# A spectral filter gated by an FFN on one Trainium2 core: slab 0 of x on the SP queue, its transposes and copies in two parts, and the statistics rows leaving from a corner of RB

## The chip, the core and the metric

The kernel runs on one core of a Trainium2 chip. A core has TensorE (PE, matmuls into PSUM; its weight loads are listed as PEld), VectorE (DVE), ScalarE (ACT), GpSimd (POOL) and SyncE (SP, which issues transfers). Each engine works through its own instructions in order, and engines wait for each other through semaphores. [...] The metric is the time on the device in microseconds (us), the median of several executions; one execution was also recorded by the profiler, and all durations come from that record.

## The reference

```python
x  = A_x                                   # 1 x 2048 x 640, bf16
xn = (x - mean(x)) / sqrt(var(x) + 1e-5)   # over the 640 columns
X  = rfft2(xn, axes=(-2, -1)) * (A_w_r + 1j * A_w_i)
s  = irfft2(X, s=(2048, 640)).astype(bf16)
f  = (gelu(xn @ w_gate) * (xn @ w_up)) @ w_down     # 640 -> 1536 -> 640, tanh form of gelu
return x + s * silu(f)
```

The branch s is a two-dimensional Fourier transform, a product with a complex weight and the way back. The branch f is a feed-forward network on the same normalised rows.

## The kernel before

x is cut into 16 slabs of 128 rows (row index n2*16 + n1: slab n1 holds every 16th row). The columns are transformed by products with cosine and sine tables, the 2048 rows as 128 x 16: a product with F1T per slab (L528), a round trip through DRAM (D2 to BU), a product with T2 (L649, L666), the row tables FM and FT (L686, L693), the weight product on VectorE (L725 to L736), and the same steps back (TI at L768, D3 to BU, I1T at L802, IT and IM at L820 and L826). The network works on four groups of 512 rows: for each of 12 column blocks a gate product into PSUM tile pg and an up product into pu (`gate_up`, L882), gelu on ACT (L899), the product of both on DVE into uT (L903), and then the down product (`down`, L966) with tanh, silu, the product with s and the sum with x.

**Who sets the order.** Nothing is scheduled by the hardware. Every step is a `Task` given to `Plan` (L115) with an engine or a choice of engines, a cost, a rank, the tasks that it comes after, and the rotating buffers (`Slot`) that it takes new or uses. `Plan.run` (L159) plays the tasks through in a simulated time, always taking the ready task of the lowest rank on a free engine, and the kernel then emits the instructions in that order. `BUFS` (L283) says how many buffers each kind has: `sp=2` PSUM tiles for transposes and transforms, `th=2`, and so on. `land` is the time at which the planner assumes that a transfer has landed. A change of costs or of `land` thus moves later instructions on all engines, though the code of those is the same.

**The start.** PE first multiplies ones by ones seven times (`keep_warm`, L362, L377) while the first loads run. Slab 0 of x is loaded from ACT's queue (L349); its task in the plan (L371) emits nothing and only carries its landing time. SP then issues slab 1, the first two column blocks of the gate weights Wg, slab 2, the first two blocks of the up weights Wu, slab 3, and the other weights, slabs and tables (L372 to L393, all by the helper at L303).

For the first group the rows are not waited for in normalised form. `turn_raw` (L452) transposes raw slabs 0 to 3 on PE, five 128 x 128 pieces each (L461), into one PSUM tile, and one copy (L463, recorded at L296, the line of `copy_on`) takes all five pieces to XR, which has a column of ones at place 128. The first two column blocks of the network (`early` in `gate_up`, L872) are computed from XR, first for slab 0 alone, with the ones column giving the column sums of the weights (WSUM); mean and 1/sigma are applied behind the product (L916, L918). Other blocks use the normalised rows xnT, transposed on PE for slabs 0 to 3 (`turn_pe`, L468) and by transfer from slab 4 on (`turn_dma`, L490).

**The statistics rows.** Mean and 1/sigma of slabs 0 to 3 stand as eight columns in RM. One transpose on PE (L560) makes eight rows of 128 of them in a PSUM tile; DVE copies these into a buffer `rt` of the kind `th` (L562); a transfer writes them to DRAM (D5, L563), and a second one reads D5 back to all 128 partitions of RB (L564). L916 and L918 read RB. Buffers of the kind `th` are also the place for the unused output of the statistics on ACT (`total` and `square`, L415 to L419) and for tanh at the end.

Of the kernel before, what the change touches and what calls it, by code (L numbers as in the profile page):

```python
# [11 lines left out]
FP32 = mybir.dt.float32  # L12
BF16 = mybir.dt.bfloat16
ACT = mybir.ActivationFunctionType
ALU = mybir.AluOpType
P = 128
S = 2048
D = 640
# [96 lines left out]
class Plan:  # L115
# [12 lines left out]
    def add(self, emit, eng, cost, rank, after=(), new=(), use=(), size=0, slow=1.0, hold=0, order=(), lag=0, land=0):  # L128
        engs = eng if isinstance(eng, dict) else {eng: cost}
        t = Task(emit=emit, engs=engs, rank=rank, after=list(after), new=list(new), size=size, slow=slow, hold=hold, order=list(order), lag=lag, land=land,  # L130
                 seq=len(self.tasks))
        for s in (*new, *use):
            s.users.append(t)
        self.tasks.append(t)
        return t
# [72 lines left out]
def c_pe(*ns):  # L208
    occ = sum(n / 2.4 + 2.5 for n in ns)
    return occ, occ + 240  # L210


def c_act(n, psum=True, extra=0):
    return 0.833 * n + 60 + extra, 0.833 * n + 200 + extra


def c_dve(n, rate=2, psum=False, extra=0):
    d = ((120 if psum else 58) + n / rate) / 0.96 + extra
    return d + 10, d + 130
# [3 lines left out]
def kernel(  # L223
# [11 lines left out]
    nc = tc.nc  # L235
    xv = A_x[0].rearrange("(n2 n1) d -> n2 n1 d", n1=NSLAB)
# [17 lines left out]
    ident = consts.tile([P, P], BF16)  # L254
# [7 lines left out]
    XR = persist.tile([P, 5, 513], BF16)  # L262
    RB = persist.tile([P, 2, 4, P], FP32)
    identF = consts.tile([P, P], FP32)
    RM = consts.tile([P, 2, 4], FP32)
    X = persist.tile([P, NSLAB, D], BF16, tag="xb", name="X")
    xnT = persist.tile([P, 5, S], BF16)
    Wg = persist.tile([P, 5, F], BF16)
    Wu = persist.tile([P, 5, F], BF16)
# [3 lines left out]
    D5 = dpool.tile([8, P], FP32)  # L273
# [12 lines left out]
    add = plan.add  # L286

    def place(slot, shape, dt=BF16):
        if slot.tag in ("sp", "pg", "pu"):
            slot.tile = psum.tile([P, *shape], dt, tag=slot.tag, name=slot.tag)  # L290
        else:
            slot.tile = work.tile([P, *shape], dt, tag=slot.tag, name=slot.tag, bufs=BUFS[slot.tag])
        return slot.tile

    def copy_on(e, out, in_):
        return nc.scalar.copy(out=out, in_=in_) if e == "ACT" else nc.vector.tensor_copy(out=out, in_=in_)  # L296
# [5 lines left out]
    def dma(out, in_, rank, size, after=(), new=(), use=(), slow=1.0, land=0):  # L302
        return add(lambda e: nc.sync.dma_start(out=out() if callable(out) else out, in_=in_() if callable(in_) else in_),  # L303
                   "SP", (430, 430), rank, after=after, new=new, use=use, size=size, slow=slow, land=land)

    gv = B_w_gate.rearrange("(c p) f -> p c f", p=P)
    uv = B_w_up.rearrange("(c p) f -> p c f", p=P)
    dv = B_w_down.rearrange("(t p) d -> p t d", p=P)
    sX = Slot("xb")
    sX.tile = X  # L310
    plan.slots["xb"].append(sX)
    x_in, g_in, u_in, tab_in, d_in = {}, {}, {}, {}, {}
# [3 lines left out]
    def load_x(a, b, land=0):  # L316
        seq[0] += 1
        t = dma(X[:, a:b, :], xv[:, a:b, :], (0, -4, seq[0]), (b - a) * 163840, use=[sX], land=land)
        for n in range(a, b):
            x_in[n] = t  # L320
# [9 lines left out]
    def load_w(sb, view, got, a, b, land=0):  # L330
        cs = slice(a * P, b * P)
        seq[0] += 1
        w = dma(sb[:, :, cs], view[:, :, cs], (0, -4, seq[0]), (b - a) * 163840, slow=1.1, land=land)
        for t in range(a, b):
            got[t] = w
# [10 lines left out]

    nc.gpsimd.memset(warm, 0.0)
    nc.vector.memset(mh, -0.5)
    nc.scalar.dma_start(out=X[:, 0, :], in_=xv[:, 0, :])  # L349
    nc.gpsimd.memset(ident, 0.0)  # L350
    nc.gpsimd.affine_select(out=ident, in_=ident, compare_op=ALU.not_equal, fill=1.0, base=0, pattern=[[-1, P]], channel_multiplier=1)
    nc.gpsimd.memset(XR[:, :, 128:129], 1.0)
# [9 lines left out]
    def keep_warm(n, after, rank=(0, -9), ns=425):  # L362
        def go(e):
            if heat.tile is None:
                place(heat, (2, 512))
            for k in range(n):
                nc.tensor.matmul(heat.tile[:, k % 2, :], lhsT=ones[:, 0:P], rhs=ones,  # L367
                                 start=True, stop=True, skip_group_check=True)
        return add(go, "PE", (n * ns, n * ns), rank, after=after, new=[] if heat.users else [heat], use=[heat] if heat.users else [])
    seq[0] += 1  # L370
    x_in[0] = add(lambda e: None, "SP", (1, 1), (0, -5), size=1, land=3620)  # L371
    load_x(1, 2, land=4150)  # L372
    load_w(Wg, gv, g_in, 0, 2, land=5210)
    load_x(2, 3, land=5700)
    load_w(Wu, uv, u_in, 0, 2, land=6760)
    load_x(3, 4, land=7250)
    t = warmed = keep_warm(7, [], ns=425)  # L377
    load_gu(2, 4)
    load_x(4, 6)
# [70 lines left out]
    raw, sums_out = {}, {}  # L450

    def turn_raw(n1):  # L452
        pt = Slot("sp")

        def half():
            return pt.tile[:, 0, :].bitcast(BF16)[:, 0:D]

        def mm(e):
            place(pt, (2, 512))
            for c in range(5):  # L460
                nc.tensor.transpose(out=half()[:, c * P:c * P + P], in_=X[:, n1, c * P:c * P + P], identity=ident)  # L461
        a = add(mm, "PE", c_pe(*[140] * 5), (0, n1), after=[x_in[n1], warmed], new=[pt], use=[sX])
        raw[n1] = add(lambda e: copy_on(e, XR[:, :, n1 * P + (n1 > 0):(n1 + 1) * P + (n1 > 0)], half().rearrange("p (c n) -> p c n", c=5)),  # L463
                      {"ACT": c_act(640)} if n1 < 1 else {"ACT": c_act(640), "DVE": (415, 560)}, None, (0, n1), after=[a], use=[pt], hold={0: 1000, 1: 1000}.get(n1, 200))
    for n1 in range(4):
        turn_raw(n1)

# [86 lines left out]
            fold(n1 // 2, [aps[n1 - 1], aps[n1]])  # L554


    sr, rt = Slot("sp"), Slot("th")

    def rows_pe(e):
        nc.tensor.transpose(out=place(sr, (2, 512))[0:8, 0, 0:P], in_=RM.rearrange("p k n -> p (k n)"), identity=identF)  # L560
    t = add(rows_pe, "PE", (215, 460), (0, 7), after=[*minused, turned[2]] + [roots[n1] for n1 in range(4)], new=[sr])
    t = add(lambda e: nc.vector.tensor_copy(out=place(rt, (P,), FP32)[0:8, :], in_=sr.tile[0:8, 0, 0:P]), "DVE", c_dve(128, 1, True), (0, 3.5), after=[t], new=[rt], use=[sr])  # L562
    rs = dma(D5, lambda: rt.tile[0:8, :], (0, -5, 0), 4096, after=[t], use=[rt])  # L563
    rb_in = dma(RB.rearrange("p k n t -> p (k n t)"), D5.rearrange("k t -> (k t)").partition_broadcast(P), (0, -5, 1), 524288, after=[rs])  # L564

    sB = Slot("xb")
# [23 lines left out]
    def rows(w, first, n, width):  # L590
        return bass.AP(tensor=w.tensor, offset=w.offset + first * L, ap=[[P * L, n], [1, width]])

    for ri, w in enumerate((A_w_r, A_w_i)):
        for G in range(8):
            b = 8 * G if G else 2
            turned_w[G].append(add(lambda e, ri=ri, w=w, G=G, b=b: nc.sync.dma_start(
                out=D4[:, b:8 * G + 8, ri, :], in_=bass.AP(tensor=w.tensor, offset=w.offset + (P - b) * L, ap=[[P * L, NSLAB], [-L, 8 * G + 8 - b], [1, LP]])),
                                   "SP", (650, 650), (2, G) if G < 2 else (3, G - 1.5), after=[turned[3]] if G < 2 else [B_in[3]], size=82432, slow=1.7))
        for a, n, b, first, width in ((0, 8, 0, 1088, LP), (8, 7, 0, 1152, LP), (15, 1, 0, 1024, LP), (0, 15, 1, P - 1, LP), (15, 1, 1, S - 1, L)):
            turned_w[0].append(add(lambda e, ri=ri, w=w, a=a, n=n, b=b, first=first, width=width: nc.gpsimd.dma_start(  # L600
                out=D4[a:a + n, b, ri, 0:width], in_=rows(w, first, n, width)), "POOL", (600, 600), (9, ri, b, a), after=[roots[15]], size=5152))
# [447 lines left out]
```

## Time and profile before

| what | value |
|---|---|
| median of 6 executions | 202.37 us (202.11 to 202.51) |
| the profiled execution | 202.31 us, of which 200.5 us are the span of its instructions |
| PE busy | 194.5 us (97%) |
| PEld, DVE, ACT, POOL busy | 118.0, 148.8, 127.1, 32.2 us |
| first and last matmul | 0.77 us; the last starts at 196.23 us |
| DMA | 32.62 MB, 163 GB/s on average over the span |

A row of the timeline or of a group reads: start, duration, engine, line, operation, output<-input, partitions x elements and type, number of instructions; in square brackets the idle time ahead of it and what ended that. A row of the waits reads: engine, what it was about to do, what it waited for, then the total in us, how often, and the longest. "PEq" is PE's own sequencer. The busy time of a matmul includes the end of its pipeline, so the time between two starts is the better measure of what one costs.

### The profile page before, as it was taken

How to read it: one execution, taken by the hardware profiler on the slowest of the kernel's cores; microseconds unless marked ns; L12 is line 12 of the kernel's file. 1: busy time of each engine (PE TensorE's matmuls, PEld its weight loads, DVE VectorE, ACT ScalarE, POOL GpSimd, SP SyncE). 2: the span in 40 equal slices, each digit the busy share in tenths (PEclk: the TensorE clock that was granted, in tenths of full speed). 3: DMA queues.
4: the chain of work that ended last, by engine and by line, in shares of the span. 5: the costliest groups of instructions: out<-in, count | busy, mean ns of one | idle time of the engine just before them, and what ended most of it. 6: DMA issues, size and time to landing. Idle time of an engine off the chain costs nothing.

```text
span 200.5 us, 4104 instructions
## 1 busy us (share of the span) xinstructions
PE 194.5 (97%) x1508; PEld 118.0 (59%) x1526; DVE 148.8 (74%) x321; ACT 127.1 (63%) x224; POOL 32.2 (16%) x71
## 2 busy tenths in 40 slices
PE   8999999999999999999999999999999999999991
PEld 3994444676444655777755455467755555457781
DVE  2898989997233159999998999933257789787774
ACT  3999879966432767777775667243466665675421
POOL 2605250697000000000000000000004022211210
PEclk9999999999999999999999999999999999999999
DMA  6999999899639767533234110117605243332432
GB/s 182 327 316 324 339 394 211 218 235 172 193 92 375 233 162 212 135 105 114 68 111 136 65 65 0 69 65 236 287 3 147 85 134 109 99 103 85 131 103 65
DMA packets 35894, 32.62 MB, mean 163 GB/s; under 512 B 10910, under 2 KB 32930, under 8 KB 35874
## 3 DMA queue, kind: packets, MB, share of 16 engines
q1 hardware_dynamic: 34434, 29.49, 50.1%
q0 software_dynamic: 1152, 2.66, 4.9%
q8 instruction: 12, 0.20, 0.4%
q10 hardware_dynamic: 288, 0.20, 0.3%
q14 instruction: 8, 0.07, 0.1%
HBM read 22.51 MB, written 9.19 MB: 158 GB/s over the span
## 4 chain that ended last, share of the span: by engine, by line
PE 96%; issue 1%; DVE 1%; ACT 0%; DVEq 0%
PE pu L882 26%; PE pg L882 25%; PE pg L966 13%; PE pu L966 13%; PE sp L693 3%; PE sp L826 3%; PE sp L768 2%; PE sp L802 2%; PE sp L666 2%; PE sp L528 2%; PE sp L367 2%; PE sp L686 1%; PE sp L820 1%; PE sp L461 1%; PE sp L474 1%
## 5 line engine op out<-in xcount | busy, mean ns | idle before, releaser
L882 PE MATMUL pu<-xnT,Wu 128*128 128x512 bf16 (+1 forms) x238 | 57.0, 365 | 0.4
L882 PE MATMUL pg<-xnT,Wg 128*128 128x512 bf16 (+1 forms) x234 | 56.5, 365 | 0.5
L903 DVE TENSOR_TENSOR uT<-pu,ge 128x512 bf16<-128x512 f32 x46 | 31.7, 690 | 20.0 <-PE pu L882 14.4
L966 PEld LDWEIGHTS <-uT 128*128 128x128 bf16 x396 | 37.8, 98 | 13.5
L899 ACT ACTIVATE ge<-pg 128x512 bf16<-128x512 f32 x46 | 27.5, 598 | 23.0 <-PE pg L882 22.2
L882 PEld LDWEIGHTS <-Wg 128*128 128x128 bf16 x285 | 25.4, 98 | 22.5 <-issue 0.3
L882 PEld LDWEIGHTS <-Wu 128*128 128x128 bf16 x285 | 24.9, 98 | 21.8
L966 PE MATMUL pg<-Wd,uT 128*128 128x320 bf16 (+2 forms) x204 | 30.7, 293 | 0.0
L966 PE MATMUL pu<-Wd,uT 128*128 128x320 bf16 (+1 forms) x192 | 29.7, 297 | 0.0
L296 ACT CAST ma<-sp 128x644 bf16<-128x644 f32 (+1 forms) x32 | 23.4, 794 | 9.7 <-PE sp L826 7.9
L928 POOL COPY xr<-s 1x1 bf16<-1x1 bf16 x1 | 0.2, 179 | 100.6 <-DVE s L852 100.6
L296 ACT CAST mc<-sp 128x640 bf16<-128x640 f32 x16 | 10.8, 696 | 5.0 <-DMA D<-mc 4.3
L929 POOL DMA_DIRECT2D xr<-in_A_x_dram x16 | 8.8, 550 | 32.3 <-DVE res L953 32.0
L975 ACT ACTIVATE th<-pu 128x320 f32<-128x320 f32 (+1 forms) x16 | 7.0, 437 | 10.9 <-PE pu L966 9.6
L980 DVE SCALAR_TENSOR_TENSOR G<-th,pg 128x320 bf16<-128x320 f32 (+1 forms) x16 | 7.7, 480 | 8.3 <-ACT th L975 8.2
L296 ACT CAST IU<-sp 128x640 bf16<-128x640 f32 x16 | 10.9, 691 | 4.1 <-PE sp L768 4.1
L296 ACT CAST Vt<-sp 128x640 bf16<-128x640 f32 x16 | 10.8, 691 | 3.7 <-PE sp L802 3.7
L975 ACT ACTIVATE th<-pg 128x320 f32<-128x320 f32 (+2 forms) x17 | 7.3, 430 | 8.3 <-PE pg L966 8.1
L980 DVE SCALAR_TENSOR_TENSOR G<-th,pu 128x320 bf16<-128x320 f32 (+1 forms) x16 | 7.7, 482 | 5.6 <-ACT th L975 5.3
L844 DVE TENSOR_TENSOR mb<-ma 128x640 bf16<-128x640 bf16 x8 | 3.9, 493 | 6.8 <-ACT ma L296 6.8
L409 DVE BATCH_NORM_STATS2 STAT<-X 128x6 f32<-128x320 bf16 x12 | 5.5, 483 | 3.8 <-DMA X<-in_A_x_dram 3.8
L746 DVE TENSOR_TENSOR R<-Y 64x644 bf16<-64x644 bf16 x16 | 7.8, 490 | 0.4
(104 smaller groups left out, 254.9 us busy)
## 6 DMA issues: line engine op xcount, KB each, us to landing
BU<-D SPq DMA_DIRECT2D x8, 640.0 KB
D<-mc SPq DMA_DIRECT2D x8, 320.0 KB
D<-IU SPq DMA_DIRECT2D x8, 320.0 KB
xr<-in_A_x_dram POOLq DMA_DIRECT2D x16, 160.0 KB, 2.6
out_dram<-res SPq DMA_DIRECT2D x15, 160.0 KB
Wg<-in_B_w_gate_dram SPq DMA_DIRECT2D x6, 320.0 KB
Wu<-in_B_w_up_dram SPq DMA_DIRECT2D x6, 320.0 KB
Wd<-in_B_w_down_dram SPq DMA_DIRECT2D x6, 320.0 KB
```

The lines of the kernel that those rows point to most:

```text
L296: return nc.scalar.copy(out=out, in_=in_) if e == "ACT" else nc.vector.tensor_copy(out=out, in_=in_)
L409: nc.vector.bn_stats(out=STAT[:, n1, 6 * g:6 * g + 6], in_=x[:, 320 * g:320 * g + 320])
L693: nc.tensor.matmul(into(q, ri), lhsT=sZ.tile[:, q, ri, :], rhs=FM[:, kinds[q][2] + (4 if ri and kind == 0 else 0), :], start=False, stop=T ...
L746: nc.vector.tensor_tensor(out=o, in0=Yf[:, ::-3, :], in1=Yf[:, 1:3, :], op=ALU.subtract)
L826: nc.tensor.matmul(into(q, s), lhsT=svs[s].tile[:, c, :], rhs=IM[:, q, :], start=False, stop=True, skip_group_check=True)
L882: nc.tensor.matmul(ps.tile[:, lo:hi + more], lhsT=w[:, c, t * P:(t + 1) * P], rhs=XR[:, c, lo + (lo > 0):hi + 1 if lo or more else hi] if ...
L899: nc.scalar.activation(out=ge.tile, in_=pg.tile if src is None else src, func=ACT.Gelu_apprx_tanh)
L903: nc.vector.tensor_tensor(out=u.tile, in0=pu.tile if src is None else src, in1=ge.tile, op=ALU.mult)
L929: nc.gpsimd.dma_start(out=sx.tile, in_=xv[:, n1, :])
L966: nc.tensor.matmul(ps.tile[:, 0:hi - lo], lhsT=uT[grp, ks[i]].tile[:, j * P:(j + 1) * P], rhs=Wd[:, ks[i], lo:hi], start=(i == 0), stop=(i ...
L975: nc.scalar.activation(out=th.tile[:, 0:hi - lo], in_=ps.tile[:, 0:hi - lo], func=ACT.Tanh, scale=0.5)
L980: nc.vector.scalar_tensor_tensor(out=G2.tile[:, lo:hi], in0=th.tile[:, 0:hi - lo], scalar=1.0, in1=ps.tile[:, 0:hi - lo], op0=ALU.add, op1 ...
```

## The change

Three edits go together.

1. Slab 0 is loaded from SP's queue as its first transfer, in place of ACT's. The assumed landing times of the first loads become 3600, 4050, 5110, 5600, 6660 and 7150 ns (before: 3620, 4150, 5210, 5700, 6760, 7250).
2. `turn_raw` treats slab 0 in two parts, pieces 0 to 2 and pieces 3 and 4. Each part has its own transposes, into its own half of the PSUM tile, and its own copy to XR. `raw[n1]` is the copy of the last part. Slabs 1 to 3 keep one part.
3. The rows of mean and 1/sigma are copied into RB[0:8, 0, 0, :], the first 128 values of RB on eight partitions, and the transfer to D5 reads them there. The buffer `rt` goes. The transfer that fills RB comes after the one that reads its corner.

```diff
-    nc.scalar.dma_start(out=X[:, 0, :], in_=xv[:, 0, :])
...
-    x_in[0] = add(lambda e: None, "SP", (1, 1), (0, -5), size=1, land=3620)
-    load_x(1, 2, land=4150)
-    load_w(Wg, gv, g_in, 0, 2, land=5210)
-    load_x(2, 3, land=5700)
-    load_w(Wu, uv, u_in, 0, 2, land=6760)
-    load_x(3, 4, land=7250)
+    load_x(0, 1, land=3600)
+    load_x(1, 2, land=4050)
+    load_w(Wg, gv, g_in, 0, 2, land=5110)
+    load_x(2, 3, land=5600)
+    load_w(Wu, uv, u_in, 0, 2, land=6660)
+    load_x(3, 4, land=7150)
...
     def turn_raw(n1):
         pt = Slot("sp")
-
-        def half():
-            return pt.tile[:, 0, :].bitcast(BF16)[:, 0:D]
-
-        def mm(e):
-            place(pt, (2, 512))
-            for c in range(5):
-                nc.tensor.transpose(out=half()[:, c * P:c * P + P], in_=X[:, n1, c * P:c * P + P], identity=ident)
-        a = add(mm, "PE", c_pe(*[140] * 5), (0, n1), after=[x_in[n1], warmed], new=[pt], use=[sX])
-        raw[n1] = add(lambda e: copy_on(e, XR[:, :, n1 * P + (n1 > 0):(n1 + 1) * P + (n1 > 0)], half().rearrange("p (c n) -> p c n", c=5)),
-                      {"ACT": c_act(640)} if n1 < 1 else {"ACT": c_act(640), "DVE": (415, 560)}, None, (0, n1), after=[a], use=[pt], hold={0: 1000, 1: 1000}.get(n1, 200))
+        parts = ((0, 3), (3, 5)) if n1 < 1 else ((0, 5),)
+        t = []
+
+        def half(k):
+            return pt.tile[:, k, :].bitcast(BF16)[:, 0:D]
+        for k, (lo, hi) in enumerate(parts):
+            def mm(e, k=k, lo=lo, hi=hi):
+                if k == 0:
+                    place(pt, (2, 512))
+                for c in range(lo, hi):
+                    nc.tensor.transpose(out=half(k)[:, c * P:c * P + P], in_=X[:, n1, c * P:c * P + P], identity=ident)
+
+            def cp(e, k=k, lo=lo, hi=hi):
+                copy_on(e, XR[:, lo:hi, n1 * P + (n1 > 0):(n1 + 1) * P + (n1 > 0)], half(k)[:, lo * P:hi * P].rearrange("p (c n) -> p c n", c=hi - lo))
+            n = hi - lo
+            a = add(mm, "PE", c_pe(*[140] * n), (0, n1), after=[x_in[n1], warmed] + t[-1:], new=[] if k else [pt], use=[sX, pt] if k else [sX])
+            t.append(a)
+            raw[n1] = add(cp, {"ACT": c_act(128 * n)} if n1 < 1 else {"ACT": c_act(128 * n), "DVE": (83 * n, 83 * n + 145)}, None, (0, n1), after=[a], use=[pt],
+                          hold=1000 if n1 < 2 else 200)
...
-    sr, rt = Slot("sp"), Slot("th")
+    sr = Slot("sp")
...
-    t = add(lambda e: nc.vector.tensor_copy(out=place(rt, (P,), FP32)[0:8, :], in_=sr.tile[0:8, 0, 0:P]), "DVE", c_dve(128, 1, True), (0, 3.5), after=[t], new=[rt], use=[sr])
-    rs = dma(D5, lambda: rt.tile[0:8, :], (0, -5, 0), 4096, after=[t], use=[rt])
+    t = add(lambda e: nc.vector.tensor_copy(out=RB[0:8, 0, 0, :], in_=sr.tile[0:8, 0, 0:P]), "DVE", c_dve(128, 1, True), (0, 3.5), after=[t], use=[sr])
+    rs = dma(D5, RB[0:8, 0, 0, :], (0, -5, 0), 4096, after=[t])
```

Because the costs, landing times and buffers of these tasks enter the plan, the emitted order changes further on as well. PE's stream is the same for the first group of transposes and products; behind that, transform groups stand up to 1.6 us of PE work earlier than before, and the instructions of DVE, ACT and SP between about 20 and 55 us change places. The last instructions of every engine are the same.

## The prediction

> **What bounds the kernel now.** I read the page first: busy shares and the chain that ended last.
>
> ```profile
> span 200.5 us, 4104 instructions
> PE 194.5 (97%) x1508; PEld 118.0 (59%) x1526; DVE 148.8 (74%) x321; ACT 127.1 (63%) x224; POOL 32.2 (16%) x71
> PE 96%; issue 1%; DVE 1%; ACT 0%; DVEq 0%
> ```
>
> TensorE (PE) is busy for 194.5 of 200.5 us and carries 96% of the chain. Then the waits of PE alone; the view has two rows in all:
>
> ```profile
> PE sp L367 <- PEq L1033: 0.8, 1, 0.8
> PE pg L882 <- ACT XR L296: 0.2, 1, 0.2
> ```
>
> So the 6.0 us in which PE is idle are 0.8 before its first instruction, 0.25 in front of the first real matmul, about 4 behind its last one (196.44 to the end), and in between some 1 us of short holes, mostly single records that are missing (two 216 ns steps in place of one). From 5.42 us on nothing that PE does was late. A new order can only keep that or spoil it; what can be gained lies in the first 7 us. The timeline of that stretch (start, duration):
>
> ```profile
> 0.72 0.41 ACTq L349 DMA_DIRECT2D X<-in_A_x_dram  x1
> 0.72 0.39 SPq L303 DMA_DIRECT2D X<-in_A_x_dram  x1
> 0.77 3.15 PE L367 MATMUL sp<-const-bfloat16-1.0 128*128 128x512 bf16 x7 [0.77 <-PEq L1033]
> 1.18 0.42 SPq L303 DMA_DIRECT2D Wg<-in_B_w_gate_dram  x1
> 2.20 0.43 SPq L303 DMA_DIRECT2D Wu<-in_B_w_up_dram  x1
> 3.90 0.89 DVE L409 BATCH_NORM_STATS2 STAT<-X 128x6 f32<-128x320 bf16 x2 [3.04 <-DMA X<-in_A_x_dram]
> 3.92 1.25 PE L461 MATMUL sp<-ident,X 128*128 128x128 bf16 x10
> 4.67 1.29 ACT L296 COPY XR<-sp 128x640 bf16<-128x640 bf16 x2 [2.02 <-PE sp L461]
> 5.42 0.90 PE L882 MATMUL pg<-XR,Wg 128*128 128x129 bf16 x10 [0.25 <-ACT XR L296]
> 6.16 0.44 PE L461 MATMUL sp<-ident,X 128*128 128x128 bf16 x5
> 6.43 0.73 PE L882 MATMUL pg<-XR,Wg 128*128 128x128 bf16 x10
> 7.07 0.74 PE L882 MATMUL pu<-XR,Wu 128*128 128x129 bf16 x10
> ```
>
> Four readings. (1) Slab 0, on ACT's queue, lands late: the trace's DMA records put the last of its 16 landings at 3.87, slab 1's on SP's queue at 3.66, and both VectorE (DVE) at 3.90 and PE at 3.92 start on slab 0. The last warm-up matmul started at 3.28 and such starts are 0.43 apart, so PE could have gone on at 3.71: 0.21 lost. (2) Ten transposes are issued 0.107 apart, until 4.97; PE then stands until 5.42 for the 0.70 us copy of slab 0 (0.45 by starts, 0.25 by the view, which counts the pipeline's tail as busy). (3) The clock: in their starts transposes of 128 columns are 0.107 apart at 4 us and 0.055 apart at 6.2; the step is at 5.81. What is gained ahead of 5.81 is gained at half speed. (4) The last pg matmul starts at 6.94, the first pu matmul could follow at 7.00, and starts at 7.07: the up weights Wu landed at 7.02. This 0.07 hole is in no view of waits, and it decides the case: whatever comes earlier ahead of it ends there.
>
> **The front, part by part.** Slab 0 moves from ACT's queue to the head of SP's. ACT's issue (0.41) goes, with no cost or gain: the table load behind it then ends near 2.0 instead of 2.44, and ACT's first copy waits for PE anyway. SP gets one issue more, so each of its loads is issued 0.46 later (0.72 to 1.18): slab 1, Wg, slab 2, Wu (2.20 to 2.66), slab 3 and the rest.
>
> Does a later issue land later? Wu was issued by 2.63 and landed at 7.02, 4.4 us on; its queue is backed up, and the DMA engines' share is 0.99 to 1.16 between 2.4 and 4.5 us. Bytes ahead of Wu's end are the same (three slabs of 160 KB, two weights of 320 KB). What differs is the ramp: from 1.74 to 2.40 queue q1 moved 39 packets and ACT's q10 11. If q1 alone moves 39, 14 KB are missing, at 330 GB/s (3.2 to 3.9 us) 0.04 us. Bounds for Wu's landing: at best nothing is missing and the round of two queues had cost something, and then PE's own chain sets the start (below, -0.26); at worst the issue sets it, +0.46. I take +0.04, since 4.4 us of backlog is far nearer to "hidden" than to "issue-bound": Wu at 7.06, Wg at 4.97 + 0.04 = 5.01.
>
> PE's own chain: slab 0, alone in its queue, lands before slab 1 did with a rival, at most 3.66, so PE transposes from 3.71. In the built order the transposes are the same ten in the same places, and ACT's first copy still waits for all five of slab 0 (PE signals once, after the fifth). So it starts 0.75 after them, as before: 4.46. Copies out of PSUM took 0.38 for 256, 0.44 for 320 and 0.70 for 640 columns; 384 columns lie near 0.49. First part done 4.95; the second starts 0.11 before that (the two copies at 4.67 overlap so) and ends at 5.22. The first three pg matmuls wait for the first part alone, the fourth for the second. With Wg at 5.01 and 0.05 to wake (7.02 to 7.07) pg starts at 5.06; the fourth, three starts on, at 5.34, after 5.22. That is 0.36 earlier than 5.42. Until 5.81 this buys 0.36 / 0.107 = 3.4 matmuls, worth 3.4 x 0.056 = 0.19 at full clock: PE is ready for pu at 7.00 - 0.19 = 6.81, which is 0.26 ahead of 7.07. Slab 2 landed at 5.64 and is wanted at 5.97: no new wait. Slab 1's copy starts about 0.07 later behind two copies' fixed costs, relative to slab 0's; slab 1's product follows at about 6.2, where that is covered. Then PE waits for Wu: 7.06 + 0.05 = 7.11. Sum of the front: +0.04 us.
>
> [...]
>
> **The rows.** Mean and 1/sigma of slabs 0 to 3 go through DRAM to all partitions (RB). Before, DVE copied them to a th buffer, whose DMA held it:
>
> ```profile
> 21.13 0.74 ACT L416 ACTIVATE th<-X 128x640 bf16<-128x640 bf16 x1 [0.63 <-DMA D<-th]
> 27.68 0.69 ACT L296 CAST mc<-sp 128x640 bf16<-128x640 f32 x1 [1.22 <-DMA D<-mc]
> 29.71 0.75 DVE L916 SCALAR_TENSOR_TENSOR IU<-RB,WSUM,IU 128x512 f32<-128x512 f32 x1 [0.35 <-DMA RB<-D]
> ```
>
> The 0.63 in the first row goes, and ACT's queue behind it (gelu, L899) comes earlier. The second row, a wait for a store, stays. On SP the small store moves ahead of one slab-pair load (issued 15.82) and RB's 512 KB ahead of one Wd load of 320 KB; RB lands about 1 us earlier, Wd's load some 1.5 later, of no matter since the down product starts at 35.8 and the last Wd landed by 33.2. The third row's 0.35 goes too. None of these was a wait of PE, so the gain is 0. The small copy itself (128 columns, 8 rows) stays.
>
> **The new order.** The first fifty-odd groups on PE are the same; behind them the planner reorders DVE, ACT and SP between about 20 and 55 us, and moves groups of the transform 0.8 to 1.6 us forward in PE's stream (the fold products near 45 us by 1.6). The cover to look at: from 30 to 45 us DVE is busy 15.00 of 15.00 us and PE 14.95. No spare engine, but the two waits that went (0.63, 0.35) lay just ahead of it. Bounds: 0 from below, as PE has nothing there to win, and from above two uT products (0.69 each) that stand before the one PE needs, 1.4. I take 0, nearest to PE's two-row list of waits. The tail is the same instructions: 0.
>
> Sum: +0.04. The profiled execution took 202.31, its span 200.5 and 1.8 around it; the median of the six is 202.37, 0.06 above. 202.37 + 0.04 is 202.4.
>
> **Rivals.** (a) Likeliest: the early work is swallowed at Wu; 202.4, its own range 202.1 to 202.7. (b) SP's issue decides: every load 0.46 later. PE would wait at Wg (5.43) and at Wu (7.48 + 0.05), +0.46, 202.8. For it: DMA ran at 260 GB/s from 4.5 to 5.4 us, so the backlog may not be solid; against: 4.4 us of it. It passes 0.2% (0.4 us) once Wu lands after 7.4. (c) The new order makes PE wait at a full DVE between 30 and 45 us: 0.7 to 1.4, 203.1 to 203.8; it decides once one uT product is due more than 0.4 late. For it: the 15.00. Against: RB is earlier. (d) Faster: the clock's step falls before 5 us, so that 0.36 counts in full, and Wu comes earlier too: 0.36 + 0.07, 201.9. Against: Wu. That the change does not do what it says belongs to (a): the split transposes release nothing earlier.
>
> **How the numbers follow.** (a) 0.50, (b) 0.15, (c) 0.21, (d) 0.14. A difference of 0.2% (0.4 us) is about what a measurement of this kernel can tell from none. (a) lies within; of (b) 0.04 and of (d) 0.01 too: same 0.55, slower 0.11 + 0.21 = 0.32, faster 0.13. The range reaches into (d) to 202.0 and into (c) to 203.2; some 0.1 is left out at each end.
>
> **What would show it.** DVE's first statistics near 3.5 instead of 3.90; the first transpose at 3.71; two copies at 4.46 and 4.84; the first pg at 5.06; the first pu still near 7.1, with a hole of about 0.25 in front of it. No ACT wait for the rows' store, no DVE wait for RB. No new row in PE's waits behind 8 us. Wrong if pu starts before 6.9 or after 7.4, or if PE's waits show ACT or DVE between 9 and 55 us.

## The result, and the profile after

The changed kernel takes 203.91 us, the median of 31 executions (202.68 to 205.10); the kernel before, run in turn with it on the same chip, takes 202.51 (67 executions, 202.06 to 204.54). The ratio is 1.006, with a 95% interval of 1.0047 to 1.0073: slower by about 1.2 us. It is not the ratio of the two medians, which differ by 1.40 us; the same holds for the ratios of the experiments. The forecast was 202.4 with a range of 202.0 to 203.2, so the result lies outside.

The profiled execution of the changed kernel took 203.92 us, span 202.1, against 202.31 and 200.5 before. First the page, then the waits of PE (the whole list):

```profile
span 202.1 us, 4105 instructions
PE 193.9 (96%) x1507; PEld 117.8 (58%) x1526; DVE 148.2 (73%) x321; ACT 126.3 (62%) x225; POOL 30.8 (15%) x71
PE 91%; DMA 4%; issue 1%; ACT 1%; DVE 1%; SPq 0%; DVEq 0%; ACTq 0%
```

```profile
PE pg L889 <- DMA Wg<-in_B_w_gate_dram: 1.4, 1, 1.4
PE sp L366 <- PEq L1040: 0.8, 1, 0.8
PE sp L535 <- ACT mc L296: 0.6, 2, 0.5
```

PE carries 91% of the chain instead of 96%; DMA has 4% of it. Two rows are new: a wait for Wg in front of the first product, and a wait for ACT's copies into mc at the product with F1T (L535; L528 before). The timeline says where they lie:

```profile
0.72 0.86 SPq L303 DMA_DIRECT2D X<-in_A_x_dram  x2
1.63 0.43 SPq L303 DMA_DIRECT2D Wg<-in_B_w_gate_dram  x1
2.67 0.43 SPq L303 DMA_DIRECT2D Wu<-in_B_w_up_dram  x1
3.04 0.89 DVE L408 BATCH_NORM_STATS2 STAT<-X 128x6 f32<-128x320 bf16 x2 [2.18 <-DMA X<-in_A_x_dram]
3.71 1.02 PE L463 MATMUL sp<-ident,X 128*128 128x128 bf16 x10
4.48 1.35 ACT L296 COPY XR<-sp 128x384 bf16<-128x384 bf16 x3 [2.26 <-PE sp L463]
6.08 0.74 PE L889 MATMUL pg<-XR,Wg 128*128 128x129 bf16 x10 [1.35 <-DMA Wg<-in_B_w_gate_dram]
7.50 0.74 PE L889 MATMUL pu<-XR,Wu 128*128 128x129 bf16 x10
29.02 0.75 DVE L923 SCALAR_TENSOR_TENSOR IU<-RB,WSUM,IU 128x512 f32<-128x512 f32 x1 [0.20 <-DMA RB<-D]
41.82 4.94 SPq L499 DMA_TRANSPOSE xnT<-s  x3
46.85 0.54 SPq L303 DMA_DIRECT2D D<-mc  x1
49.97 1.29 ACT L296 CAST mc<-sp 128x640 bf16<-128x640 f32 x2 [2.23 <-DMA D<-mc]
```

What was gained early is there: statistics at 3.04 instead of 3.90, transposes at 3.71 instead of 3.92, the first copy at 4.48. Then PE waits until 6.08 for Wg, whose last part lands at 6.03 (4.97 before) by the trace's landing records, and pu starts at 7.50 (7.07), with Wu landed at 7.46 (7.02). That is **0.43 us** at the front.

The last three rows are the second place. Here are the same three instructions of the kernel before:

```profile
41.85 2.56 SPq L492 DMA_TRANSPOSE xnT<-s  x2
44.50 0.54 SPq L303 DMA_DIRECT2D D<-mc  x1
48.65 1.29 ACT L296 CAST mc<-sp 128x640 bf16<-128x640 f32 x2 [1.24 <-DMA D<-mc]
```

ACT's copies need an mc buffer, of which there are two, and the buffer is free when the store D<-mc has landed. After, that store stands on SP behind three transposes instead of two, is issued 2.35 us later, and the copies start 1.3 later. The third transpose is also a long one: by its own record it takes 2.28 us, where the two ahead of it take 1.24 and 1.23. SP's list of waits puts that down to VectorE:

```profile
SPq L499 <- DVE G L987: 3.8, 3, 2.3
```

So of the 2.35 us about 1.3 are one more transpose in front of the store, and about 1.05 are that transpose waiting for VectorE. PE runs out of PSUM tiles at 49.96 and 50.93: holes of 0.63 and 0.32 us in its starts (before there is one of 0.06). From the first pu to the last matmul it is 190.06 us instead of 189.16, **0.90** more. From the start of the last matmul to the end of the span it is 4.59 us instead of 4.29, **0.30**, in the copies and stores at the end, which I followed no further (the run `after_mended` below has the same 4.59). 0.43 + 0.90 + 0.30 = 1.63, the difference of the two spans.

Why Wg is late shows in the stretches of the first microseconds (columns: stretch and its length, busy time of PE, PEld, DVE, ACT, POOL, granted clock, busy share of the DMA engines, GB/s). Before:

```profile
3.00:3.80 0.80, 0.80 (x3) 0.00 (x1) 0.00 (x0) 0.00 (x0) 0.00 (x0) 1.00 1.08 334
3.80:4.60 0.80, 0.79 (x8) 0.68 (x8) 0.70 (x2) 0.00 (x0) 0.00 (x0) 1.00 1.14 337
```

After:

```profile
3.00:3.80 0.80, 0.80 (x4) 0.24 (x3) 0.76 (x2) 0.00 (x0) 0.00 (x0) 1.00 0.69 156
3.80:4.60 0.80, 0.80 (x11) 0.75 (x9) 0.73 (x4) 0.12 (x1) 0.16 (x1) 1.00 0.93 282
```

Both slabs are in by 3.54, and until Wg's packets come in numbers the DMA engines move 156 GB/s instead of 334. The traces' records of single packets say more. Wg has 640 packets of 512 bytes, and the first of them ends between 2.75 and 3.04 us in all fifteen profiled executions of this study, whether Wg is issued at 0.72 or at 1.64. What differs is how many follow: between 3.2 and 3.6 us 231 packets of this size end in the kernel before and 90 in the changed one. In the nine executions with Wg issued by 1.18 there are 213 to 259 of them, in the six with Wg issued at 1.53 or later 88 to 136. The late issue thus shows as a thin flow in a half-empty transfer path, and not as a shift of the whole load; why the flow is thin is not shown. (334 - 156) x 0.8 and (337 - 282) x 0.8 are 186 KB less by 4.6 us; between 2.0 and 3.0 us the changed kernel moved 43 KB more (290 against 247 GB/s over the stretch). On balance 143 KB are missing at 4.6 us, 0.42 us at 337 GB/s. That this is close to Wu's delay (0.44) fits, but is no proof: 39 KB are made up by 5.4 us and lost again by 7.0.

### The profile page after: what moved, and what is told of

Same layout as the page of the kernel before. It is cut to its first block, busy times and chain, and to the rows that moved or that the text cites. A ratio compares the mean times of both kernels' runs of the same rounds, so it can differ in the third digit from the quotient of the medians.

```text
span 202.1 us, 4105 instructions
## 1 busy us (share of the span) xinstructions
PE 193.9 (96%) x1507; PEld 117.8 (58%) x1526; DVE 148.2 (73%) x321; ACT 126.3 (62%) x225; POOL 30.8 (15%) x71
## 4 chain that ended last, share of the span: by engine, by line
PE 91%; DMA 4%; issue 1%; ACT 1%; DVE 1%; SPq 0%; DVEq 0%; ACTq 0%
PE pu L889 26%; PE pg L889 25%; PE pg L973 12%; PE pu L973 12%; PE sp L700 3%; PE sp L833 3%; PE sp L775 2%; PE sp L809 2%; DMA Wg<-in_B_w_gate_dram 2%; PE sp L673 2%; DMA D<-mc 2%; PE sp L535 1%; PE sp L827 1%; PE sp L693 1%; ACT mc L296 1%
## 5 line engine op out<-in xcount | busy, mean ns | idle before, releaser
L889 PE MATMUL pg<-xnT,Wg 128*128 128x512 bf16 (+1 forms) x232 | 55.9, 365 | 0.5
L906 ACT ACTIVATE ge<-pg 128x512 bf16<-128x512 f32 x46 | 28.0, 610 | 25.1 <-PE pg L889 23.5
L296 ACT CAST Z<-sp 128x1024 bf16<-128x1024 f32 x8 | 7.9, 1017 | 2.5 <-PE sp L673 2.5
L415 ACT ACTIVATE th<-X 128x640 bf16<-128x640 bf16 x10 | 7.7, 787 | 0.7 <-DMA X<-in_A_x_dram 0.7
```

The costliest lines, as they stand in the source:

```text
L415: nc.scalar.activation(out=place(junk, (D,)), in_=x, func=ACT.Copy, scale=-1.0 / D, accum_out=less)
L889: nc.tensor.matmul(ps.tile[:, lo:hi + more], lhsT=w[:, c, t * P:(t + 1) * P], rhs=XR[:, c, lo + (lo > 0):hi + 1 if lo or more else hi] if ...
L906: nc.scalar.activation(out=ge.tile, in_=pg.tile if src is None else src, func=ACT.Gelu_apprx_tanh)
```

## The experiments

My theory after this comparison: two losses. (F) Slab 0 at the head of SP's queue makes Wg and Wu late, because their issue is late. (S) The new order of SP's queue makes the store near 45 us late. Times are given against the kernel before, run in turn on the same chip; "first pu" and the like are of the profiled execution.

**Each loss alone.** In `x0_on_sp` the kernel before has only slab 0's transfer moved:

```diff
-    nc.scalar.dma_start(out=X[:, 0, :], in_=xv[:, 0, :])
...
-    x_in[0] = add(lambda e: None, "SP", (1, 1), (0, -5), size=1, land=3620)
+    x_in[0] = add(lambda e: nc.sync.dma_start(out=X[:, 0, :], in_=xv[:, 0, :]), "SP", (1, 1), (0, -5), size=1, land=3620)
```

> The kernel before with one thing changed: slab 0 is the first transfer of SP's queue instead of ACT's; every other instruction and its order are as before. Theory (what a load on SP is delayed by is the place of its issue in SP's queue, and the first Wg decides): Wg's last part lands near 6.0 instead of 4.97, the first pg product starts near 6.1 instead of 5.42, the first pu near 7.5 instead of 7.07; +0.4 us on the kernel before. Rival 1 (the prediction's term, a later issue hides in the backlog): Wg near 5.0, pu near 7.1, +0.04. Rival 2 (the late landing of Wg in the one profiled execution was an accident of that execution): Wg anywhere between, and a mean near 0.

Measured: 203.41 against 202.57, ratio 1.0038 (1.0016 to 1.0061). Wg landed at 5.62, Wu at 7.91.

```profile
5.67 1.27 PE L881 MATMUL pg<-XR,Wg 128*128 128x129 bf16 x10 [0.69 <-DMA Wg<-in_B_w_gate_dram]
6.73 0.74 PE L460 MATMUL sp<-ident,X 128*128 128x128 bf16 x5
7.26 1.27 PE L881 MATMUL pg<-XR,Wg 128*128 128x128 bf16 x10
8.33 1.29 PE L881 MATMUL pu<-XR,Wu 128*128 128x129 bf16 x10
```

(F) stands and the prediction's +0.04 falls. But pu comes at 8.33, later than Wu: ten products take 1.27 here and 0.74 in the changed kernel. The clock's step, which I read from the starts (0.107 apart, then 0.055), is at 9.72 in this execution; it was at 5.81 before and at 4.32 in the changed kernel. I come back to that.

`x0_back_on_act` is the reverse: the changed kernel, its order kept, with slab 0 on ACT's queue.

```diff
+    nc.scalar.dma_start(out=X[:, 0, :], in_=xv[:, 0, :])
...
-    load_x(0, 1, land=3600)
+    seq[0] += 1
+    x_in[0] = add(lambda e: None, "SP", (430, 430), (0, -4, seq[0]), size=163840, land=3600, use=[sX])
```

> The changed kernel with slab 0 back on ACT's queue and nothing else undone; the order of all engines stays that of the changed kernel. Theory (two separate losses, 0.43 at the front and about 0.95 at 50 us from the order of SP's queue): Wg lands near 5.0, pg starts at 5.06 (split copies), pu near 7.1; the stall of PE behind ACT's mc copies near 50 us stays; 0.4 less than the changed kernel, 0.8 to 1.0 more than before. Rival (the stall at 50 us follows from the late front, through what is shifted against SP's transfers): the stall goes too and the time is that of before within 0.2 us.

Measured: 203.32 against 202.57, 1.0037 (1.0012 to 1.0062). Wg landed at 4.91, pg started at 5.29, pu at 6.86; from pu to the last matmul 189.70, 0.54 more than before.

```profile
PE pg L891 <- ACT XR L296: 0.2, 1, 0.2
PE sp L537 <- ACT mc L296: 0.2, 1, 0.2
```

The third row of the list is the start of the program, as before. The row for Wg is gone, the row for mc is not: (S) is no consequence of (F) alone. It is smaller here: the third transpose takes 1.23 us by its record instead of 2.28, and the store is issued at 45.31.

`store_one_earlier` takes the place of the store in SP's queue by itself:

```diff
-        for t in plan.run():
+        order = plan.run()
+        late = [t for t in order if t.on == "SP"]
+        late = late[late.index(stored[4]) - 1]
...
+        order.remove(late)
+        order.insert(order.index(stored[4]) + 1, late)
+        for t in order:
```

> The changed kernel with two neighbours of SP's queue exchanged near 44 us: the store D<-mc that stood behind three xnT transposes stands behind two of them, as in the kernel before; all other engines keep their order. Theory (this store holds the mc buffer that ACT's copies near 50 us wait for): the store is issued about 2.3 us earlier (near 44.6 instead of 46.85), ACT's copies start 1.2 us earlier, PE's holes at 50 us go; 0.8 to 1.0 less than the changed kernel, that is 0.4 to 0.6 above before. Rival (a full DVE or the order of ACT makes PE wait, and the store is only the last of several): the holes stay within 0.3 us, and so does the time.

Measured: 203.30 against 202.57, 1.0030 (1.0011 to 1.0050).

```profile
41.45 2.56 SPq L499 DMA_TRANSPOSE xnT<-s  x2
44.10 0.54 SPq L303 DMA_DIRECT2D D<-mc  x1
49.14 1.29 ACT L296 CAST mc<-sp 128x640 bf16<-128x640 f32 x2 [1.50 <-DMA D<-mc]
```

The store is issued 2.75 us earlier, the copies start 0.83 earlier, and of PE's two holes one of 0.22 is left. The store took 4.96 us to its last landing (44.10 to 49.06), against 3.04 in the changed kernel and 4.08 in the kernel before; the DMA engines' busy share over these stretches is 1.15, 0.93 and 1.10, so the earlier store probably shares them with more. So I expected too much of it (0.8 to 1.0); by the ratios it is worth about 0.3% of the 0.6%, with intervals that would allow 0.1 to 0.5%.

`all_edits_old_order` has the three edits in the order of before (the planner keeps the old tasks, costs and landing times; only what they emit changes):

```diff
+            copy_on(e, XR[:, 0:3, 0:P], half()[:, 0:384].rearrange("p (c n) -> p c n", c=3))
+            copy_on(e, XR[:, 3:5, 0:P], pt.tile[:, 1, :].bitcast(BF16)[:, 0:256].rearrange("p (c n) -> p c n", c=2))
...
-    t = add(lambda e: nc.vector.tensor_copy(out=place(rt, (P,), FP32)[0:8, :], in_=sr.tile[0:8, 0, 0:P]), "DVE", c_dve(128, 1, True), (0, 3.5), after=[t], new=[rt], use=[sr])
+    t = add(lambda e: nc.vector.tensor_copy(out=RB[0:8, 0, 0, :], in_=sr.tile[0:8, 0, 0:P]), "DVE", c_dve(128, 1, True), (0, 3.5), after=[t], new=[rt], use=[sr])
```

> All three edits (slab 0 on SP, transposes and copies of slab 0 in two parts, rows from the corner of RB) in the order of instructions that the kernel before has. Theory: only the front's loss is left, +0.4 us on the kernel before, with no stall near 50 us. Rival 1 (an edit costs something by itself, beyond the late Wg): more than +0.6. Rival 2 (the split saves what the late Wg costs): within 0.1 us of before.

Measured: 203.08 against 202.57, 1.0029 (1.0003 to 1.0054). Wg landed at 5.97, pu started at 7.55. The split and the corner of RB add nothing that can be measured to slab 0's move. The expectation "no stall near 50 us" missed: there is a hole of 0.32 at 50.4. That spot is close to critical in the old order too: `x0_x1_exchanged` and `x0_x1_on_act` below, also in the old order, have two holes each there, of 0.22 and 0.32 and of 0.29 and 0.32.

**Is it the place of the issue?** `tiny_first` leaves slab 0 on ACT's queue and puts 128 bytes ahead of SP's loads.

```diff
+    SC = consts.tile([P, 64], BF16)
...
-    x_in[0] = add(lambda e: None, "SP", (1, 1), (0, -5), size=1, land=3620)
+    x_in[0] = add(lambda e: nc.sync.dma_start(out=SC[0:1, :], in_=xv[0:1, 0, 0:64]), "SP", (1, 1), (0, -5), size=1, land=3620)
```

> The kernel before with one transfer more: 128 bytes of x into an unused corner, issued by SP ahead of its other loads; slab 0 stays on ACT's queue, and all else is as before. It moves next to no bytes, but each load of SP is issued one place later. Theory (the place of the issue in SP's queue sets the landing): Wg lands at 5.3 to 6.0 instead of 4.97, Wu at 7.3 to 7.6 instead of 7.02, and the time is 0.4 to 0.8 above before. Rival (what delays Wg is that slabs 0 and 1 leave one queue in place of two, or the order of the bytes): Wg within 0.15 of 4.97, time within 0.2 us of before.

Measured: 203.97 against 202.52, 1.0069 (1.0042 to 1.0095). Wg was issued at 1.53 and landed at 5.79, Wu at 7.55.

```profile
5.84 0.74 PE L883 MATMUL pg<-XR,Wg 128*128 128x129 bf16 x10 [0.86 <-DMA Wg<-in_B_w_gate_dram]
7.60 0.74 PE L883 MATMUL pu<-XR,Wu 128*128 128x129 bf16 x10 [0.17 <-DMA Wu<-in_B_w_up_dram]
```

```profile
3.00:3.80 0.80, 0.80 (x4) 0.24 (x2) 0.67 (x2) 0.00 (x0) 0.00 (x0) 1.00 0.61 144
```

128 bytes in the way of an issue do what the whole slab did, the half-empty stretch (144 GB/s) included. Slab 1, which is also issued later here (1.11 instead of 0.72), lands no later (3.49, 3.66 before): it is the weights that suffer. A DVE wait of 0.48 us near 30 us comes on top in this execution (mb, in front of a product with F1T), which I have no cause for.

`x0_x1_exchanged` (with the copies in two parts) gives SP slab 0 and ACT slab 1, so that Wg keeps its place:

```diff
-    nc.scalar.dma_start(out=X[:, 0, :], in_=xv[:, 0, :])
+    nc.scalar.dma_start(out=X[:, 1, :], in_=xv[:, 1, :])
...
-    x_in[0] = add(lambda e: None, "SP", (1, 1), (0, -5), size=1, land=3620)
-    load_x(1, 2, land=4150)
+    x_in[0] = add(lambda e: nc.sync.dma_start(out=X[:, 0, :], in_=xv[:, 0, :]), "SP", (1, 1), (0, -5), size=1, land=3620)
+    seq[0] += 1
+    x_in[1] = add(lambda e: None, "SP", (430, 430), (0, -4, seq[0]), size=163840, land=4150, use=[sX])
```

> Order of before, copies of slab 0 in two parts, slab 0 first on SP's queue and slab 1 on ACT's in its place: the issue of Wg and of all behind it stays where it was (1.18, 1.64, 2.20). Theory (place of the issue): Wg near 4.97, Wu near 7.0; slab 0 lands by 3.7, pg starts near 5.06, pu near 7.07; within 0.2 us of before. Rival (slab 0 on SP is what delays the weights, wherever the others stand): Wg after 5.3, Wu after 7.3, 0.4 to 0.8 above before.

Measured: 202.56 against 202.52, 0.9997 (0.9978 to 1.0016). Wg was issued at 1.17 and landed at 4.71, Wu at 7.05.

```profile
4.76 0.74 PE L889 MATMUL pg<-XR,Wg 128*128 128x129 bf16 x10 [0.45 <-DMA Wg<-in_B_w_gate_dram]
7.09 0.74 PE L889 MATMUL pu<-XR,Wu 128*128 128x129 bf16 x10 [0.51 <-DMA Wu<-in_B_w_up_dram]
```

```profile
3.00:3.80 0.80, 0.80 (x7) 0.24 (x6) 0.26 (x1) 0.00 (x0) 0.00 (x0) 1.00 1.09 331
```

So slab 0 on SP harms nothing as long as Wg is issued in time, and the prediction's reading 4 is seen in full here: PE is early, and what it gained ends at Wu. Over all fifteen profiled executions the landing of Wg falls into two groups that do not meet: 4.71 to 4.97 with Wg issued by 1.18, 5.38 to 6.03 with it issued at 1.53 or later. For Wu the groups are 6.81 to 7.29 and 7.35 to 7.91 (without the two runs below that issue Wu ahead of slab 2).

`x0_x1_on_act` goes the other way, both slabs on ACT's queue and Wg first on SP's:

```diff
     nc.scalar.dma_start(out=X[:, 0, :], in_=xv[:, 0, :])
+    nc.scalar.dma_start(out=X[:, 1, :], in_=xv[:, 1, :])
...
-    load_x(1, 2, land=4150)
+    seq[0] += 1
+    x_in[1] = add(lambda e: None, "SP", (430, 430), (0, -4, seq[0]), size=163840, land=4150, use=[sX])
```

> Order of before, copies of slab 0 in two parts, and slabs 0 and 1 both on ACT's queue, so that Wg is the first load of SP and each of SP's loads is issued 0.46 earlier. Theory (place of the issue): Wg lands near 4.5, Wu near 6.5; the first pg product starts at 5.0 to 5.1 behind the first copy, pu at 6.7 to 6.8, 0.2 to 0.4 less than before. Rival 1 (the backlog of bytes sets Wu's landing): Wu within 0.15 of 7.02, pu at 7.0 to 7.1, time of before. Rival 2: slab 0 now shares the engines with Wg's small packets and lands after 4.2, pg starts after 5.5, slower by 0.1 to 0.3.

Measured: 203.75 against 202.52, 1.0033 (1.0005 to 1.0060). My theory missed. The executions lie in two groups, five from 202.16 to 203.04, the profiled one among them, and seven from 203.61 to 204.11, so what follows is of the lower group. Wg was issued at 0.72 and landed at 4.96, Wu was issued at 1.79 and landed at 7.01, as in the kernel before, and slab 1 came last (5.42):

```profile
5.46 0.45 PE L463 MATMUL sp<-ident,X 128*128 128x128 bf16 x5 [0.79 <-DMA X<-in_A_x_dram]
```

An earlier issue buys nothing here, for Wu as the first rival had it. That pg started only at 5.75 is the second rival's loss with another cause: slab 0 landed at 3.91, and PE stood in front of slab 1, whose transposes precede pg. The stretch from 3.0 to 3.8 moves 330 GB/s, as before; that with a full path the bytes decide is likely and not shown apart, since one slab less stands in front of Wg in this run. As far as these runs reach, the place of the issue matters in one direction: 0.72 and 1.18 give the same landing of Wg, 1.53 and later a later one.

**Is that all?** `after_mended` keeps every edit and the new order, and takes both causes away: slab 1 goes to ACT's queue as above, and one pair of slabs gets a buffer of the kind IU, idle then, in place of mc:

```diff
                 if s == 0:
-                    place(A, (2, D))
+                    if j == 6:
+                        A.tile = work.tile([P, 2, D], BF16, tag="IU", name="IU", bufs=2)
+                    else:
+                        place(A, (2, D))
```

> The changed kernel with all its edits and its order, and two mends: slab 1 goes to ACT's queue in slab 0's old place (so Wg and all behind it are issued as early as before), and the outputs of the seventh pair of slabs near 50 us go to a buffer of the kind IU, which is idle then, in place of the third use of the two mc buffers. Theory (late issue of the weights, and the mc buffer held by a late store, are the two losses and all of them): Wg near 4.9, pu near 7.07, no hole over 0.1 us between 44 and 56 us, time within 0.2 us of before. Rival (the new order has a further price, a full DVE or ACT): 0.4 us or more above before.

Measured: 202.50 against 202.62, 0.9999 (0.9983 to 1.0015). PE's list of waits has only the start of the program left, and between 44 and 56 us no hole above 0.05:

```profile
PE sp L367 <- PEq L1045: 0.8, 1, 0.8
```

From pu to the last matmul it is 189.17. The two causes together are the whole 0.6%, within 0.15%. (pg started at 5.01; Wu landed at 7.29 and pu started at 7.33 in this execution, later than the 7.07 expected.) The buffer of its own takes the wait away whatever holds the store; what puts the store late is read from `store_one_earlier` and from SP's queue.

**The clock.** In the profiled executions with an early step of the clock, pu is 0.3 to 0.5 us late by (F); over all executions (F) costs 0.6 to 0.8 (`all_edits_old_order` and `x0_on_sp`; `tiny_first`, with its further wait, 1.4). What was left was PE's idle time in front of Wg. `x0_on_sp_filled` has three more products of ones there; if the idle time makes the upper five of the twelve executions of `x0_on_sp` (203.91 to 204.22, the others 203.13 to 203.49), they should go:

```diff
+            if n1 == 1:
+                for k in range(3):
+                    nc.tensor.matmul(pt.tile[:, 1, :], lhsT=ones[:, 0:P], rhs=ones, start=True, stop=True, skip_group_check=True)
```

> Slab 0 on SP in the order of before (as the run x0_on_sp), and three more products of ones by ones (512 columns, not used) on PE behind slab 1's transposes, so that PE works while it waits for Wg. [...]

Measured: 202.74 against 202.52, 1.0026 (1.0000 to 1.0051), where the kernel without the filling had 1.0038. Eight of twelve executions lie between 202.2 and 203.0, below all twelve of `x0_on_sp` (203.13 and up), though pu started at 7.49 in the profiled one; four lie between 203.3 and 204.5. The upper executions did not go away, so this run does not decide. `warm_up_of_four` is the cleaner test: the kernel before with an idle stretch of PE that nothing waits for.

```diff
-            for k in range(n):
+            for k in range(4):
```

> The kernel before with four products of ones at the start in place of seven: PE stands idle from about 2.5 to 3.9 us, and nothing waits for these products, so the loads, copies and the starts of pg (5.42) and pu (7.07) stay where they were. Theory (an idle stretch of PE of about a microsecond early on puts off the clock's step in many executions, and each microsecond at half clock behind pu costs half a microsecond): the step near or behind 7.3, median 0.3 to 1.0 above before with a wide spread. Rival (the spread of the changed kernel has nothing to do with PE's idle time): step at 4 to 6 us as in the other runs, time of before within 0.15.

Measured: 203.68 against 202.54, 1.0052 (1.0032 to 1.0072), executions from 202.94 to 204.33. Wg landed at 4.92 and Wu at 7.05, as before; PE:

```profile
4.01 1.25 PE L461 MATMUL sp<-ident,X 128*128 128x128 bf16 x10 [1.38 <-DMA X<-in_A_x_dram]
5.50 1.24 PE L882 MATMUL pg<-XR,Wg 128*128 128x129 bf16 x10 [0.25 <-ACT XR L296]
7.07 1.27 PE L882 MATMUL pg<-XR,Wg 128*128 128x128 bf16 x10
8.14 0.90 PE L882 MATMUL pu<-XR,Wu 128*128 128x129 bf16 x10
```

The slabs, Wg, Wu and the copies are in time; ten products take 1.24 and 1.27 us instead of 0.73, until the clock steps up at 8.49, and pu starts 1.07 us late. (The 7.3 expected for the step was an estimate of mine that no run shows.) In this execution three warm-up products less, and with them an idle stretch of 1.4 us early in the program, thus cost about a microsecond through the clock alone; the ratio says the same over all eight. For the changed kernel this is the likely reason of its wide spread (it stands idle for 1.35 us), but its own profiled execution had the step early, at 4.32, so for it this is argued and not shown.

**Can it be made to pay?** `exchanged_own_buffer` is the exchange of the slabs with the IU buffer, in the order of before (both diffs above).

> The order of before, slabs 0 and 1 exchanged between the queues, copies of slab 0 in two parts, and the buffer of kind IU for the seventh pair near 50 us. The run with the exchange alone had a hole of 0.33 us at 50.1 us behind the same mc copies, so the spot is close to critical in the old order too. Theory: the hole goes, 0.1 to 0.4 us below the exchange alone, so 0 to 0.4 below before. Rival (the holes near 50 us are filled by work that waits elsewhere, or an IU buffer is wanted): time of before within 0.15.

Measured: 202.38 against 202.62, 0.9994 (0.9977 to 1.0010): the holes at 50 us are gone (from pu to the last matmul 189.10), but no gain is established. `wu_ahead_of_x2` goes on from it and issues Wu ahead of slab 2:

```diff
+        order.remove(x_in[2])
+        order.insert(order.index(u_in[0]) + 1, x_in[2])
+        for k, lo, t in ((0, 128, 0), (0, 128, 1), (1, 0, 0), (1, 0, 1)):
+            order.remove(piece[k, lo, t])
+            order.insert(order.index(flip[2]), piece[k, lo, t])
```

> As the run with the exchange and the own buffer, with Wu issued ahead of slab 2, and on PE slab 1's pg products and slab 0's pu products ahead of slab 2's transposes. Theory (once PE's own chain is early, Wu's landing is what decides the front): Wu lands near 6.5 in place of 7.05, pu starts near 6.6, slab 2 lands near 7.0 just as its transposes are due; 0.4 to 0.5 below the run without it. Rival (slab 2 takes the place of Wu: its statistics stand ahead of the copies on ACT, so the copies of slabs 2 and 3 come 1 us later and PE waits for them between 7 and 11 us): the gain is given back, between 0 and +0.8.

Measured: 203.16 against 202.62, 1.0036 (1.0022 to 1.0049); the rival was right. Wu landed at 6.40 and pu started at 6.46, 0.61 earlier than before, but slab 2 landed at 6.83, and ACT's statistics and copy of it came so late that PE had holes of 0.68 at 7.6 and 0.28 at 9.4:

```profile
6.46 0.73 PE L893 MATMUL pu<-XR,Wu 128*128 128x129 bf16 x10
7.03 0.77 PE L462 MATMUL sp<-ident,X 128*128 128x128 bf16 x10
8.32 0.44 PE L482 MATMUL sp<-ident,s 128*128 128x128 bf16 x5 [0.52 <-ACT XR L296]
```

`wu_ahead_copies_in_time` moves the products behind these holes one group later:

```diff
+        for n1 in range(2):
+            pe = [t for t in order if t.on == "PE"]
+            nxt = piece[1, 128, 1] if n1 == 0 else pe[pe.index(normal[n1]) + 1]
+            order.remove(normal[n1])
+            order.insert(order.index(nxt) + 1, normal[n1])
```

> As the run with Wu ahead of slab 2, but on PE the transposes of the normalised slabs 0 and 1 stand one group later, behind slab 1's pu products and behind the next pg products, so that the PSUM tiles that they wait for (held by ACT's copies of slabs 2 and 3) are free by then. Theory: the holes of 0.68 us at 7.6 and 0.28 us at 9.4 go, pu starts at 6.5, the last matmul starts 0.8 earlier than in that run, and the time is 0.3 to 0.5 below before (near 202.1 where before has 202.5). Rival (another late piece of slab 2, its statistics, takes their place near 11 us): holes of 0.3 or more at 9 to 13 us, time of before or above.

Measured: 202.96 against 202.54, 1.0017 (1.0004 to 1.0030). Holes of 0.29 at 7.8 and 0.38 at 9.5 remain, and the gain of 0.47 at pu (6.60) is given back. No version was found that beats the kernel before.

## Why the prediction was wrong

- **The step that failed** is the term for Wu's landing, "14 KB are missing ... 0.04 us", with its reason, "4.4 us of backlog is far nearer to 'hidden' than to 'issue-bound'". Measured in its place: Wg +1.06, Wu +0.44, first pu +0.43. The 4.4 us were Wu's, read from its issue to its landing, and I took all of it for a queue. For Wg, two places ahead, only two slabs stand in front (320 KB, 1.0 us at 330 GB/s). In the kernel before Wg's packets came in numbers from 3.2 on, while the slabs ended (slab 1 landed by 3.66); with the issue 0.45 later less than half as many come between 3.2 and 3.6, and the path stands half empty. That the later issue does this is shown; by what means is open. The row to read was the first transfer behind the slabs, not the last one of the queue.
- Rival (b), "SP's issue decides", had the mechanism, at 0.15. Its price for Wu (7.48) is what was measured (7.46), with some luck: in the five other runs with late issues Wu landed between 7.35 and 7.91. For Wg (5.43) it was too low (6.03, and 5.38 to 5.97 in four other runs with slab 0 on SP). Its +0.46 for the front compares with 0.43 in the profiled execution. What it left out is the clock: in `x0_on_sp`, with PE idle for 0.7 us in front of Wg, the step came only at 9.72.
- **The second failed step** is "I take 0" for the new order, with its place, 30 to 45 us and DVE. DVE is again busy for 15.00 of 15.00 us there, and PE waits for nothing. The loss came at 50 us, from a store behind transposes on SP. The row that carries it was in the prediction, one instance earlier: "27.68 ... mc<-sp ... 1.22 <-DMA D<-mc", of which I wrote "stays". The same wait stands at 48.65 in the kernel before (1.24), where PE already lost 0.06, and I did not follow SP's queue there. Rival (c) had the right size by luck (0.7 to 1.4; measured 0.90, and 0.54 without the late front) and the wrong place: VectorE enters only by way of SP, where the transpose that waits for it holds the store back.
- PE's own chain was right where Wg was in time: pg at 5.01 and 5.04 in `after_mended` and `exchanged_own_buffer` against 5.06 forecast, the copies in `after_mended` at 4.48 and 4.86 against 4.46 and 4.84, its transposes at 3.71. That pu then waits for Wu was right too (0.51 us in `x0_x1_exchanged`). For a step of the clock before 5 us, on which rival (d) rests, the kernel before shows nothing (5.81); the changed kernel had it at 4.32, and what PE gained ended at Wg.
- The rows: ACT's wait of 0.63 for the store of th is gone, as forecast, and DVE's wait for RB fell from 0.35 to 0.20 instead of going. Both are worth nothing to PE, as forecast.
- Slab 0 landed at 3.01, sooner than "at most 3.66". That was no gain: PE's warm-up ended at 3.71.
- The result is the sum of two rivals that were weighed as exclusive. The range held each (202.8, and 203.1 at the low end) and not both.

## What to carry to other kernels

Ahead of moving a transfer into a queue, look at each transfer behind it, the first one above all, and not only at the last: how long do the transfers in front of it keep the path busy, and do its own packets flow by then? Here two slabs kept it busy until about 3.5 us, and Wg, issued 0.35 to 0.46 us later, did not follow in numbers. When a plan is replayed with new numbers, follow every wait for a store or a buffer that is already long in the old trace through the new order of the issuing queue, since it may need little more to reach PE: here one more transpose in front of the store, and that transpose's wait for VectorE, took ACT's wait from 1.24 to 2.23 us, and PE had holes of 0.63 and 0.32 us instead of 0.06.

## What the runs showed of the hardware

The weights Wg and Wu, issued 0.35 to 0.48 us later, landed 0.3 to 1.1 us later in six profiled executions; slab 1, issued 0.39 to 0.46 later in the same six, landed no later (3.49 to 3.58 against 3.66). Wg issued 0.46 earlier landed no sooner (4.96 against 4.97). A transfer of 128 bytes held the loads behind it back by 0.35 us in issue and Wg by 0.82 in landing. The parts of one load can spread: Wg's sixteen parts landed between 4.45 and 4.97 before, and between 4.36 and 6.03 after. A half-empty path is not the only place for that: in `after_mended` Wg's parts landed between 4.26 and 4.76, but slab 2's between 4.74 and 6.22.

The step of PE's clock lay between 3.46 and 6.73 us in thirteen of the profiled executions of this study, and at 8.49 and 9.72 in two that had PE idle for 1.4 us (`warm_up_of_four`) and 0.7 us (`x0_on_sp`) ahead of it. An idle stretch does not always put it off: `tiny_first`, idle for 0.9 us, and `all_edits_old_order`, idle for 1.0, were at full speed with their first pg product (5.84 and 6.02). The granted clock in the stretches of the profile shown above is 1.00, those ahead of the step included; only the distance of the starts shows the step (in the kernel before 0.107 us, then 0.055). The step moves from execution to execution, between 3.46 and 9.72 us; what sets its time was not shown here.
